# Linear attention followed by a squared-ReLU FFN on one core: first k by hardware queues, transposes in pieces, q by whole rows, squares on two engines

## The chip, the cores and the metric

The kernel runs on one core of a Trainium2 chip. TensorE (PE) multiplies matrices, VectorE (DVE) and ScalarE (ACT) do the work on elements, GpSimd (POOL) issues the loads that cast fp32 to bf16, SyncE (SP) issues stores and crossbar transposes. The metric is the device time of one execution in microseconds.

## What is computed

For each of 8 batches and 8 heads, 576 positions of 64 values are projected to 128 features, and exp of plus and minus the projection gives 256 features. The attention is linear: keys and values are summed once, queries read the sum. The result, 4608 tokens of 512, goes through an FFN of width 2048 whose activation is the square of a ReLU.

```python
def phi(x):
    proj = np.einsum('bhsd,df->bhsf', x, w_phi)
    proj = proj - np.max(np.abs(proj), axis=-1, keepdims=True)
    return np.concatenate([np.exp(proj), np.exp(-proj)], axis=-1)
q_p, k_p = phi(q), phi(k)
kv = np.einsum('bhsf,bhsd->bhfd', k_p, v)
z = np.sum(k_p, axis=2)
num = np.einsum('bhsf,bhfd->bhsd', q_p, kv)
den = np.einsum('bhsf,bhf->bhs', q_p, z)[..., None] + 1e-06
# x = num / den, heads side by side: (4608, 512)
h = np.maximum(x @ w_in, 0.0)
out = (h * h) @ w_out
```

Inputs and output are fp32.

## The kernel before

**Work of one batch.** `attention(b)` works on one batch at a time. q, k and v come to SBUF as bf16 tiles `xq`, `xk`, `xv` (two buffers each) of 128 partitions; the first 512 positions of a head lie four to a partition, and the last 64 positions of all heads form a small extra part, "s". A tile holds 18 blocks of 128 columns. They are transposed into `kT` and `qT`: for batches 0 and 1 on TensorE (`pe_transposes`, L616, with a copy out of PSUM by VectorE or ScalarE, L439 or L441), for later batches by one crossbar DMA for a whole tile on SyncE's queue (`transposed`, L626).

k is projected in five groups (L642, in batch 0 L670, matmuls on 64 rows of the array in pairs), VectorE takes the largest magnitude (L722, L677) and ScalarE the two exponentials `kp` and `kn` (L728, L705). `em_ops` and `v_ops` put the factor of the maximum on v (L740, L747, L762, L766), and `kv_ops` sums keys times values on TensorE (L783, L788) and copies the sum to `kv`. For q, `qmax_ops` finds the maxima (L642 or L816, then L823), `q_ops` makes the features (L858, exponentials L873) in five chunks `c`, and `out_ops` multiplies by the sums (L888), scales (L900), divides (L908, L912) and transposes the result into `xT`, on TensorE in batch 0 (L928, L937) and by crossbar DMAs of four blocks later (L950).

**FFN.** Tokens go in nine chunks of 512: eight are the main parts of the batches, the ninth holds all the small parts (`xS`). `ffn_in` (first chunk: `ffn_in_small`, L1049) multiplies by w_in (L1038); `relu_sq` takes the ReLU out of PSUM on ScalarE (L1015) or VectorE (L1017) into one of four buffers `hr` and squares it on VectorE (L1024) into `h2`. `ffn_out` multiplies by w_out (L1103), a copy brings the result to one of three `ot` buffers, and SyncE stores it (L1121).

**What sets the order.** Nothing is scheduled on the chip. `Plan` collects all operations with what they read and write; `Machine.run` plays them through with a cost for each and a due time from the list `KEYS`, and the program then issues each engine's instructions in the order that came out. `pin` holds that order. Each engine executes its list strictly in order, SyncE and GpSimd too, so that an instruction that waits holds all behind it. `STATES` says for each operation that two engines can do which one does it (`plan.either`). `RELEASES` hold loads back until a ScalarE instruction has ended. `SLACK` is what the planner adds to the expected landing of a DMA. In the first 45 us, where the planner finds TensorE idle and a PSUM bank is free, matmuls on a zero tile `warm` fill the time (L1195); how many is fixed when the program is built.

**Loads.** All loads but w_phi are issued by GpSimd, which casts in the DMA: `load` (L512 main part, L520 small part), `load_q` (L532), the FFN weights L581 and L587. `load_q` reads each q row of 256 fp32 values in two halves of 128, for both pairs of positions `jj`, so that the blocks of one `jj` lie together:

```python
out=x[:, jj * 1024 + a * 256 : jj * 1024 + z * 256].rearrange("p (h x) -> p h x", x=128),
in_=q[b][2 * a : 2 * z, 0:512, :].rearrange("h (p j) d -> p h (j d)", j=4)[:, :, jj * 128 : jj * 128 + 128]))
```

In batch 0, a chunk of q then needs one half of the columns for all eight heads. Only w_phi comes by hardware queues, one half issued on SyncE and the other on ScalarE (L476).

## Time and profile before

| what | value |
|---|---|
| time, three runs | 361.73, 362.86, 364.84 us; median 362.86 |
| profiled execution | 362.49 us, its span 360.4 us |
| mean granted TensorE clock | 0.986 |
| busy: PE, DVE, ACT, POOL | 346.7, 292.5, 231.9, 112.5 us |
| DMA packets under 512 bytes | 77249 of 102632 |
| SyncE's instructions: whole transposes of q and k, 4-block ones of xT, small ones of xS | 12, 28, 7 |

The span runs from the first to the last instruction of the profiled execution. "Busy" counts the time in which at least one instruction of the engine was in progress; matmuls are pipelined and overlap, so a busy TensorE isn't one that does as much as it could. The groups give the sum of busy time of like instructions, the mean of one, and the engine's idle time just before them with what ended it. The granted clock is the share of TensorE's full clock that it was given.

### The profile page before, as it was taken

Reading aid. Unit: us, or ns where it says so; the run is one execution under the profiler, and the core shown is the slowest. Engines: PE = TensorE matmul, PEld = TensorE weight load, DVE = VectorE, ACT = ScalarE, POOL = GpSimd, SP = SyncE. Lnnn points to the kernel's source line nnn. Section 1 sums busy time; section 2 is a strip of 40 time slices with the busy share of each in tenths; the row PEclk is TensorE's granted clock in tenths of the full one; section 3 lists DMA queues with packets and bytes.
Section 4 is the critical chain, followed back from the end, with each engine's and each line's share of the span. In section 5 each row is a group of like instructions: output and inputs, shape, how many; then the busy total and the mean of one; then the engine's idle time right before and its main releaser. Section 6 shows DMA issues by size and latency. Waiting matters only on the chain.

```text
span 360.4 us, 8594 instructions
## 1 busy us (share of the span) xinstructions
PE 346.7 (96%) x3442; PEld 198.0 (55%) x3442; DVE 292.5 (81%) x503; ACT 231.9 (64%) x434; POOL 112.5 (31%) x167
## 2 busy tenths in 40 slices
PE   8579999999999999999999999999999999999995
PEld 8368886554554555446544555565455554444444
DVE  4998999899999977899789888999788965686131
ACT  2986899598888783959677847957785340310310
POOL 8626727366636951363415212010000000000000
PEclk9959999999999999999999999999999999999999
DMA  8999999998999999898847774447230031100213
GB/s 96 194 201 136 188 182 117 169 150 107 164 154 126 153 129 188 167 139 121 98 102 96 128 98 104 93 69 122 81 96 2 17 95 45 36 0 2 112 33 89
DMA packets 102632, 39.62 MB, mean 110 GB/s; under 512 B 77249, under 2 KB 98113, under 8 KB 102593
## 3 DMA queue, kind: packets, MB, share of 16 engines
q0 software_dynamic: 51744, 18.36, 47.3%
q1 hardware_dynamic: 50608, 20.55, 25.4%
q8 instruction: 27, 0.44, 0.5%
q10 hardware_dynamic: 240, 0.16, 0.2%
q14 instruction: 13, 0.10, 0.1%
HBM read 36.77 MB, written 9.44 MB: 128 GB/s over the span
## 4 chain that ended last, share of the span: by engine, by line
PE 75%; DVE 11%; ACT 9%; issue 2%; DMA 1%; POOL 0%; DVEq 0%; POOLq 0%; ACTq 0%
PE psum L1103 29%; PE psum L1038 24%; PE psum L888 5%; PE psum L783 4%; DVE mq L823 4%; PE psum L642 3%; PE psum L858 3%; PE psum L1049 2%; ACT kp L728 2%; DVE mk L722 2%; DVE va L766 2%; ACT kn L728 2%; DMA xq<-in_q_dram 1%; DVE h L1024 1%; PE psum L1067 1%
## 5 line engine op out<-in xcount | busy, mean ns | idle before, releaser
L1103 PE MATMUL psum<-wout,h 128*128 128x512 bf16 x560 | 131.5, 379 | 0.0
L1038 PE MATMUL psum<-xT,win 128*128 128x512 bf16 x448 | 105.0, 379 | 0.6 <-ACT hr L1015 0.4
L1015 ACT ACTIVATE hr<-psum 128x512 bf16<-128x512 f32 x91 | 53.6, 598 | 49.7 <-PE psum L1038 26.1
L1103 PEld LDWEIGHTS <-h 128*128 128x128 bf16 x560 | 50.7, 98 | 56.9 <-issue 2.7
L1038 PEld LDWEIGHTS <-win 128*128 128x128 bf16 x512 | 47.5, 98 | 53.6 <-issue 1.6
L1024 DVE TENSOR_TENSOR h<-hr 128x512 bf16<-128x512 bf16 x144 | 56.9, 416 | 16.2 <-ACT hr L1015 15.3
L873 ACT ACTIVATE qp<-psum 128x1024 bf16<-128x1024 f32 (+1 forms) x40 | 37.3, 938 | 20.0 <-PE psum L858 17.4
L532 POOL DMA_DIRECT2D xq<-in_q_dram x52 | 37.6, 726 | 39.1 <-ACT hr L1015 10.3
L823 DVE TENSOR_REDUCE mq<-psum 128x8 f32<-128x1024 f32 (+1 forms) x40 | 43.7, 1110 | 4.6 <-PE psum L642 3.7
L1017 DVE TENSOR_SCALAR hr<-psum 128x512 bf16<-128x512 f32 x53 | 36.1, 683 | 9.8 <-PE psum L1038 8.3
L722 DVE TENSOR_REDUCE mk<-psum 128x8 f32<-128x1024 f32 (+1 forms) x35 | 38.1, 1108 | 2.4 <-PE psum L642 1.7
L728 ACT ACTIVATE kp<-psum 128x1024 bf16<-128x1024 f32 (+1 forms) x35 | 32.8, 937 | 10.2 <-DVE mk L722 10.2
L766 DVE TENSOR_TENSOR va<-xv,va 128x1024 bf16<-128x1024 bf16 (+1 forms) x36 | 38.6, 1101 | 0.6 <-ACT va L747 0.4
L873 ACT ACTIVATE qn<-psum 128x1024 bf16<-128x1024 f32 (+1 forms) x40 | 37.4, 940 | 2.0 <-PE psum L888 2.0
L900 DVE TENSOR_TENSOR psum<-psum,en 128x520 f32<-128x520 f32 (+1 forms) x40 | 27.9, 700 | 7.4 <-PE psum L888 6.4
L728 ACT ACTIVATE kn<-psum 128x1024 bf16<-128x1024 f32 (+1 forms) x35 | 32.9, 948 | 0.1
L912 DVE TENSOR_TENSOR xo<-psum,rden 128x512 bf16<-128x512 f32 (+1 forms) x40 | 27.3, 687 | 0.9
L512 POOL DMA_DIRECT2D xv<-in_v_dram x26 | 18.9, 727 | 28.9 <-ACT qp L873 10.5
L512 POOL DMA_DIRECT2D xk<-in_k_dram x28 | 20.2, 721 | 21.9 <-ACT va L747 7.4
L783 PE MATMUL psum<-va,kp 128*128 128x65 bf16 x256 | 21.1, 199 | 0.1
L783 PE MATMUL psum<-va,kn 128*128 128x65 bf16 x256 | 20.9, 198 | 0.1
L441 ACT ACTIVATE ot<-psum 128x512 f32<-128x512 f32 x24 | 14.4, 603 | 10.0 <-PE psum L1103 6.8
(68 smaller groups left out, 407.4 us busy)
## 6 DMA issues: line engine op xcount, KB each, us to landing
out_dram<-ot SPq DMA_DIRECT2D x32, 256.0 KB, 2.6
xk<-in_k_dram POOLq DMA_DIRECT2D x26, 128.0 KB, 4.4
xv<-in_v_dram POOLq DMA_DIRECT2D x24, 128.0 KB, 4.4
xq<-in_q_dram POOLq DMA_DIRECT2D x48, 64.0 KB, 3.4
win<-in_moe_w_in_dram POOLq DMA_DIRECT2D x4, 512.0 KB, 11.0
wout<-in_moe_w_out_dram POOLq DMA_DIRECT2D x4, 512.0 KB, 7.7
xq<-in_q_dram POOLq DMA_DIRECT2D x4, 256.0 KB, 7.5
xv<-in_v_dram POOLq DMA_DIRECT2D x2, 512.0 KB, 8.5
```

Source lines behind the costliest of these rows:

```text
L512: pin(nc.gpsimd.dma_start(out=x[:, a * 512 : z * 512].rearrange("p (h x) -> p h x", x=4 * D), in_=src[b][2 * a : 2 * z, 0:512, :].rearrang ...
L532: pin(nc.gpsimd.dma_start(out=x[:, jj * 1024 + a * 256 : jj * 1024 + z * 256].rearrange("p (h x) -> p h x", x=128), in_=q[b][2 * a : 2 * z ...
L722: pin(nc.vector.tensor_reduce(out=mk_view(g), in_=ps2(pj)[:, :, : n * Fd].rearrange("p e (i f) -> p e i f", f=Fd), axis=AX.X, op=ALU.max, ...
L728: pin(nc.scalar.activation(out=dst[slot][:, :, :n, :].rearrange("p e i f -> p e (i f)"), in_=ps2(pj)[:, :, : n * Fd], func=ACT.Exp, scale= ...
L766: pin(nc.vector.tensor_tensor(out=o[:, :, :D], in0=xv[s2][:, 512 * g0 : 512 * g1].rearrange("p (m d) -> p m d", d=D), in1=o[:, :, D].to_br ...
L783: pin(nc.tensor.matmul(out=o[:, sg, hi, :], lhsT=(kp, kn)[sg][kgroup[pr]][:, j % 2, 2 * hi + j // 2, :], rhs=va[s2][sg_of(sg, pr)][:, 8 * ...
L823: pin(nc.vector.tensor_reduce(out=mqb[:, c, :, :n], in_=ps2(pj)[:, :, : n * Fd].rearrange("p e (i f) -> p e i f", f=Fd), axis=AX.X, op=ALU ...
L873: pin(nc.scalar.activation(out=o, in_=i_, func=ACT.Exp, scale=sgn))
L1015: pin(nc.scalar.activation(out=hr[sl], in_=ps1(g), func=ACT.Relu))
L1024: pin(nc.vector.tensor_tensor(out=dst, in0=i_, in1=i_, op=ALU.mult))
L1038: pin(nc.tensor.matmul(out=o, lhsT=win[mc // 4][:, kc, mc % 4 * P : (mc % 4 + 1) * P], rhs=x, start=(kc == 0), stop=(kc == KC - 1)))
L1103: pin(nc.tensor.matmul(out=ps1(g), lhsT=h2[c % 2][mc // 4][:, mc % 4, tt * P : (tt + 1) * P], rhs=wout[mc // 4][:, mc % 4, :], start=(mc = ...
```

## The change

**First k.** Batch 0's k groups 0 and 1 and its small part are copied as fp32 by hardware queues into the three `ot` buffers, which are not in use yet; three copies on VectorE or ScalarE cast them into `xk`. SyncE issues group 0, one half of w_phi and the small part, ScalarE group 1 and the other half of w_phi. GpSimd loads only groups 2 and 3 of that k.

**q by whole rows.** `load_q` is gone; q is loaded by `load` as k is, in rows of 256 values, so block `2 * h + jj` belongs to head `h`. `q_ts` and the views of `qT` step by two blocks. A chunk of q in batch 0 now needs both halves of the q load, in which the halves are heads 0 to 3 and 4 to 7.

**Transposes in pieces.** `transposed` issues five crossbar DMAs for a tile, four of four blocks and one of two, each waiting for its own part of the load. Batch 1's q goes this way too, and is no longer transposed on TensorE (`PE_Q`).

**Squares.** The square in `relu_sq` may be done by ScalarE.

**Planner.** PSUM bank 7 is kept free until 27 us of the planner's time, so fill matmuls can stand wherever TensorE is idle there. `SLACK` is smaller, limits and patience are others, and `KEYS`, `STATES` and `RELEASES` are new lists. By the built programs, 69 of the 144 squares are on ScalarE; VectorE has 8 more copies of key-value sums, 5 more of `ot` and 5 more ReLUs; the fill matmuls are 210 instead of 118; GpSimd issues 24 main loads of q in place of 48 for batches 2 to 7; SyncE's transposes of q and k are 65 instead of 12.

```diff
-SLACK = {"first": 1.2, "v0": 2.5, "ld": 0.8, "x": 1.2, "kq": 1.0}
+SLACK = {"first": 0.6, "v0": 1.0, "ld": 0.6, "x": 0.8, "kq": 1.0}
...
-        self.free_at = [0.0] * self.BANKS
+        self.free_at = [0.0] * (self.BANKS - 1) + [RESERVED]
...
+            if name == "PE" and t < RESERVED:
+                spare = self.BANKS - 1
...
+    kf = {0: ot[0], 1: ot[1], "s": ot[2]}
...
+    def first_k(g, name, e, lat):
+        def fn():
+            pin(e.dma_start(
+                out=kf[g].rearrange("p (h x) -> p h x", x=4 * D),
+                in_=k[0][2 * g : 2 * g + 2, 0:512, :].rearrange("h (p j) d -> p h (j d)", j=4)))
+        first_ops.append(add(name, (0.6, lat), -10, fn, w=[("ot", g)], what="xk"))
...
+    first_k(0, "SP", nc.sync, 2.9)
+    first_w(1, "ACT", nc.scalar)
+    first_w(0, "SP", nc.sync)
+    for hi in range(2):
+        first_s(hi, "SP", nc.sync, 3.0)
+    first_k(1, "ACT", nc.scalar, 3.6)
+
+    for n, g in enumerate((0, 1, "s")):
+        def fn(g=g):
+            if g == "s":
+                copy(xk[0][:, 2048:2304], kf[g][:, :256])
+            else:
+                copy(xk[0][:, g * 512 : g * 512 + 512], kf[g])
+        x = 256 if g == "s" else 512
+        o = add("DVE", dve_cost(x), -9 + n * 0.1, fn, r=[("ot", n)],
+                w=[("xk", 0, "s", hi) for hi in range(2)] if g == "s" else [("xk", 0, g)], what="kc")
+        plan.either((o, "ACT", act_cost(x)))
...
-            def fn():
-                pin(nc.sync.dma_start_transpose(out=xt, in_=x))
-            add("SP", (2.8 if tag == "xk" else 3.4, 0), key, fn, r=of(tag, b, (0, 1, "s") if tag == "xq" else (0, 1, 2, 3, "s")),
-                w=[(ttag, s2, t) for t in range(18)], dma=(3.6, HW_IN, "x", "kq"), what="X" + tag)
+            def piece(a, n, srcs):
+                def fn():
+                    pin(nc.sync.dma_start_transpose(out=xt[:, a : a + n, :], in_=x[:, a * P : (a + n) * P]))
+                add("SP", (1.23, 0), key + a * 0.1, fn, r=of(tag, b, [u for u in srcs if u == "s"]) + [t for t in srcs if t != "s"],
+                    w=[(ttag, s2, t) for t in range(a, a + n)], dma=(0.2 * n, HW_IN, "x", "x"), what="X" + tag)
+            for g in range(4):
+                piece(4 * g, 4, [(tag, s2, g)])
+            piece(16, 2, ["s"])
...
-            return [8 * (c // 2) + h for h in range(8)] if first else [8 * (c // 2) + 4 * (c % 2) + i for i in range(4)]
+            return [2 * h + c // 2 for h in (range(8) if first else range(c % 2 * 4, c % 2 * 4 + 4))]
...
-            pin(nc.vector.tensor_tensor(out=dst, in0=i_, in1=i_, op=ALU.mult))
-        add("DVE", dve_cost(256), key, fn, r=[("hr", sl)], w=toks, what="sq")
+            if now[0].eng == "ACT":
+                pin(nc.scalar.activation(out=dst, in_=i_, func=ACT.Square))
+            else:
+                pin(nc.vector.tensor_tensor(out=dst, in0=i_, in1=i_, op=ALU.mult))
+        o = add("DVE", dve_cost(256), key, fn, r=[("hr", sl)], w=toks, what="sq")
+        plan.either((o, "ACT", act_cost(512)))
...
-    load(k, xk, 0, -9, "xk", prs=((0, 1),))
...
-    load(k, xk, 0, -8, "xk", prs=((1, 2), (2, 4)), single=False)
-    load_q(0, -7.5, jjs=(0,), single=False)
+    load(k, xk, 0, -8, "xk", prs=((2, 4),), single=False)
+    load(q, xq, 0, -7.5, "xq", prs=((0, 2), (2, 4)))
     load_v0(-7)
-    load_q(0, -6, jjs=(1,))
...
-    load_q(1, -3.9)
+    load(q, xq, 1, -3.9, "xq", prs=((0, 2), (2, 4)) if 1 not in K["PE_Q"] else ((0, 4),))
...
-                load_q(b, r, release=max(r, 1.0), prs=PIECES)
+                load(q, xq, b, r, "xq", prs=PIECES, release=max(r, 1.0))
...
+    'PE_Q': [0],
...
-    'LIM': {'b0': 7, 'att': 3, 'kv': 7, 'op': 6},
-    'AHEAD': 356.131,
-    'PATIENCE': 60.701,
+    'LIM': {'tp': 6, 'att': 6, 'kv': 6, 'op': 4},
+    'AHEAD': 168.898,
+    'PATIENCE': 15.023,
```

## The prediction

> **What bounds the kernel now.** I read the busy shares first, then the stretches of ten microseconds, then the timeline of the start, and only then the groups.
>
> ```profile
> PE 346.7 (96%) x3442; PEld 198.0 (55%) x3442; DVE 292.5 (81%) x503; ACT 231.9 (64%) x434; POOL 112.5 (31%) x167
> ...
> PE   8579999999999999999999999999999999999995
> ...
> PEclk9959999999999999999999999999999999999999
> ```
>
> TensorE is busy almost everywhere, except in the first tenth. But pipelined matmuls overlap in this view, so I counted its work by start-to-start distances in dense stretches of the trace: 0.216 us for 512 columns, 0.056 for 128, 0.0295 for 65, 0.057 for 130, 0.109 for 256; matmuls on 64 rows run in pairs at half of that. 1072 of 512 columns in the two FFN layers are 231.6 us, the 256 small ones of the first chunk 14.3, the last 32 3.5; the attention's 512 and 64 of its key-value sums 18.7, its 640 output matmuls 18.9, projections and features 25, transposes 5. A change between 64-row and full matmuls costs 0.095 more (89 of them, from 60 us on: 0.092 to 0.096), and the order has 112: 10.6. The sum is 327.5 us. The last matmul ends at 356.4, so **28.9 us are TensorE's idle time**, and only that and the 4 us behind it can change much.
>
> ```profile
> 0.00:10.00 10.00, 8.79 (x104) 8.07 (x105) 5.01 (x12) 3.35 (x5) 8.92 (x17) 1.00 0.95 105
> 10.00:20.00 10.00, 5.19 (x75) 3.66 (x72) 9.50 (x17) 9.96 (x25) 6.03 (x9) 0.81 1.44 197
> 20.00:30.00 10.00, 8.43 (x138) 7.55 (x138) 8.83 (x15) 7.93 (x21) 3.14 (x5) 0.67 1.32 175
> 30.00:40.00 10.00, 10.00 (x199) 9.30 (x197) 9.64 (x25) 7.23 (x13) 7.71 (x11) 1.00 1.24 159
> ```
>
> The columns are PE, PEld, DVE, ACT, POOL, granted clock, DMA. Most of the 8.79 in the first row is fill work. From 10 to 20 ScalarE has no free moment and VectorE hardly any; from 20 to 30 the clock is at 0.67. By single microseconds it is 0.50 from about 16.4 to 26.7, after four (13 to 17) with TensorE busy 0.90, 0.00, 0.40 and 0.26.
>
> ```profile
> 2.70 5.38 DMA xq<-in_q_dram
> ...
> 7.70 0.60 ACT L705 ACTIVATE kp<-psum 128x512 bf16<-128x512 f32 x1 [5.07 <-PE psum L670]
> ...
> 27.51 0.39 ACT L441 ACTIVATE kv<-psum 128x260 bf16<-128x260 f32 x1
> ...
> 33.20 0.61 PE L1049 MATMUL psum<-xT,win 128*128 128x128 bf16 x8
> ```
>
> These four rows, one from the chain of waits and three from the timeline, are the start: ScalarE's first exponential at 7.70, the last key-value copy at 27.51 (done 27.9), the first FFN matmul at 33.20. TensorE's work ahead of that matmul adds up to about 12.3 us, so **21 us of the 28.9 lie ahead of it, 8 behind**. From there TensorE is dense.
>
> **The change part by part.** Work: batch 1's q is no longer transposed on TensorE, 18 x 0.056 = 1.0 us less. The changed program's order has 122 changes of mode instead of 112: 10 x 0.095 = 1.0 more. The two cancel. Ahead of the first FFN matmul the new order has 12.6 us of real work instead of 12.3, no difference worth a term. So all turns on idle time.
>
> *First k by hardware queues.* Before, k's first 128 KB piece was issued on GpSimd at 2.00 and used at 6.25. Now 256 KB of fp32 start on SyncE and on ScalarE's queue at 0.74. Nearest rows: hardware copies of 256 KB land 2.6 us after issue, w_phi's 32 KB in 2.1 to 2.5; a software load of 256 KB takes 5.8 and is the other end. I take 2.9: 3.6 us. w_phi is now second on both queues (0.58 each), so its cast (0.39, done about 4.2) stands ahead of the k casts in VectorE's order. An fp32 cast of 512 columns is not in the trace; bounds are a quarter-size cast at 0.39 and a 512-column fp32 copy at 0.69; I take 0.6, behind idle VectorE (3.67 to 6.73 before), except for the first, which is on the path: 4.8. Four cold transposes (0.107 each) and latency: ScalarE starts the kT copies at about 5.4 (4.8 to 7.7 by the ends).
>
> *ScalarE's list up to the last key-value copy* in the new order: 16 exponentials of 512 at 0.475 start to start, 7 of 1024 at 0.90, 4 of 256 at 0.27, 7 copies at 0.49, 12 small ones at 0.155, 3 key-value copies at 0.28, 3 of 8 columns at 0.16: 21.6 us. 5.4 + 21.6 = 27.0. The second half of k and the q halves still come by GpSimd; among its loads they stand third, fifth and sixth, and I add 0.5 for one of them being late: 27.5, against 27.9. The gain is small since before, a part of the list came later.
>
> *From there to the first FFN matmul* it took 5.3 us. VectorE's order there held a qT copy, a maximum and a kT copy (0.2 + 0.6 + 0.33) between the scalings and the xT copies; the new order has none of them: 4.2, so 31.7. **Ramp: 33.2 - 31.7 - 0.3 (more work done) = 1.2, and 0.6 for the half clock**: the 64 key-value matmuls took 2 us more than at full clock (1.05 per pair for 0.55), partly on the path; now 210 fill matmuls instead of 118, 89 of them in the two stretches where TensorE stood idle, should hold the clock. If it falls all the same, these 89 take 0.107 instead of 0.056 each, 4.5 us on the path. Ends: no gain if k lands like a software load; 3.7 if nothing is late and ScalarE starts at 4.8.
>
> *Squares on ScalarE.* 69 of 144 move; 51 stand ahead of the last batch's exponentials.
>
> ```profile
> L1024 DVE TENSOR_TENSOR h<-hr 128x512 bf16<-128x512 bf16 x144 | 56.9, 416 | 16.2 <-ACT hr L1015 15.3
> L1015 ACT ACTIVATE hr<-psum 128x512 bf16<-128x512 f32 x91 | 53.6, 598 | 49.7 <-PE psum L1038 26.1
> ```
>
> A square costs 0.416 on VectorE; on ScalarE the nearest row is the relu of that size, 0.598. VectorE loses 69 x 0.416 = 28.7 and gains about 11 (8 key-value copies, 5 ot copies and 5 relus more, fewer transposes' copies): 292 to 275. ScalarE goes from 232 to about 262. Between 40 and 110 us VectorE is busy 78 to 100% and TensorE idles 3.4 by the count above; with both engines near 80%, I take 2.5 of the 8 us back, with ends of 6 gained and 3 lost (a square that waits behind exponentials of 1.03). By these rows a square is 1.4 times dearer on ScalarE, which had 128 us free. The Trainium skill, page "ScalarE: Activation LUTs", "Rules for kernel authors", speaks against this part: multiplications belong on VectorE, up to about three times faster in bf16; by that ratio the 69 squares would cost 57 us more engine time than they do now. One table load stands in the built program before and after, so Square costs no reload.
>
> *Whole q rows.* In the trace's DMA records a 256-byte packet takes 41 ns, a 512-byte one 60: the q data of one batch saves 27% of its DMA time. It is hidden after 46 us, and helps the loads of the start (DMA at 1.2 to 1.4 there). I cost it at nothing.
>
> *Crossbar pieces.* A whole q or k transpose holds SyncE 3.1 us and lands after 5.2 to 6.5; one of four blocks, as xT has it, 1.2 and 2.6. A tensor goes from 3.1 to 4 x 1.20 + 1.17 = 6.0 us of SyncE, 13 tensors instead of 12: 78 instead of 37, with 42 for xT and xS. SyncE has the room. The same skill's "DMA: Bandwidth & Descriptors", "Bandwidth", warns that small transfers are descriptor-dominated; it measured loads, no row here shows that for transposes. Every piece waits in SyncE's order for its part of a load, and stores and xT transposes stand behind it. Before, such a wait reached 3.6 us (at 58.5) with TensorE covered by FFN work.
>
> **Sum.** Ramp -1.8, steady idle -2.5, work 0: 360.4 - 4.3 = 356.1 of span. Around it lie 2.1 us (362.49 - 360.4): **358.2 us**. The profiled run stands 0.4 below the median, 362.86.
>
> **Rivals.** *The start gives more* (0.17): ScalarE starts at 4.8, no load is late (3.7), and balanced engines leave TensorE 2 of its 8 us: 362.5 - 3.7 - 6 = 353. For it: VectorE 81%, ScalarE 64%. Against it: TensorE already dense behind 33 us.
> *It moves and nothing comes of it* (0.28): k early, but the q halves and k's second half, still on GpSimd behind 512 KB of v, hold ScalarE as long; the steady gain is 1: 361.5. For it: 5.38 us for q in the chain; DMA at 1.4.
> *SyncE's queue becomes the bound* (0.14, slower): 65 pieces wait in order; where a load is over some 4 us late, the xT transposes behind it start the next chunk late, and TensorE's FFN backlog runs out. At 2 us in each of five batches, 10 us: 358.2 + 10 = 368. Against it: no TensorE wait on a DMA after 20 us in the list of waits.
> *The forecast* has 0.41, from 355 to 360.5.
>
> The measurement tells about 1% (3.6 us) from no change. Faster by more than that is all of the first rival and most of the forecast: 0.54; within: 0.32; slower: 0.14. The range leaves out the best end and most of the slow rival: 353 to 366.
>
> **What would show it.** Right: first exponential at about 6, clock 1.0 from 16 to 27, first FFN matmul at 31 to 32, VectorE near 275 and ScalarE near 262 us, no TensorE wait on xT. Wrong: loads of q or k in the chain beyond 10 us, a half clock with the longer fill, an idle stretch of TensorE between 60 and 290 that xT ends, or ScalarE as the releaser of most waits.

## The result and the profile after

The changed kernel takes 375.03 us, the median of four runs (372.89 to 377.88), against 362.86 before: a ratio of 1.0334, 95% interval 1.0251 to 1.0418. I had forecast 358.2. The profiled execution took 374.58 us with a span of 372.8. Times here are medians of all executions of a kernel, while the ratios leave out single executions that ran in a slower state.

The first lines are of the profile page of the changed kernel: busy times, then TensorE and its clock in 40 slices.

```profile
PE 354.8 (95%) x3516; PEld 201.7 (54%) x3516; DVE 277.6 (74%) x448; ACT 261.8 (70%) x487; POOL 92.7 (25%) x139
...
PE   4699899999999999989999999999999999999995
...
PEclk9599999999999999999999999999999999999999
```

VectorE and ScalarE came out as forecast (277.6 and 261.8 us; 275 and 262), and TensorE's work hardly changed. What changed is its idle time. Counted by start-to-start distances in both traces, with 0.11 us for a change between 64-row and full matmuls, it is 28.0 us before and 40.6 after (the prediction summed the work with 0.095 and had 28.9 before), and these 12.6 us are the whole difference. By stretch: up to 40 us it idles 29.4 us instead of 21.8, from there to the end 11.2 instead of 6.2. The stretches of ten microseconds (PE, PEld, DVE, ACT, POOL, granted clock, DMA, GB/s):

```profile
0.00:10.00 10.00, 4.53 (x43) 4.10 (x43) 3.29 (x9) 0.00 (x0) 6.53 (x13) 0.91 0.86 141
10.00:20.00 10.00, 7.62 (x93) 7.23 (x93) 2.86 (x7) 7.42 (x15) 4.87 (x7) 0.57 1.37 200
20.00:30.00 10.00, 9.71 (x159) 7.99 (x157) 9.78 (x17) 9.74 (x27) 2.71 (x4) 1.00 1.20 162
30.00:40.00 10.00, 9.02 (x160) 6.73 (x157) 9.00 (x13) 9.95 (x18) 6.56 (x10) 1.00 1.27 161
```

In the first ten microseconds ScalarE does nothing at all, although the DMA moves more than before (141 GB/s, 105 before). The half clock, forecast to go, only moved: 0.57 from 10 to 20 and 1.00 from 20 to 30, where it was 0.81 and 0.67. The reason is in the timeline of the start:

```profile
5.20 0.28 DVE L517 CAST wphi<-wphi_f 128x128 bf16<-128x128 f32 x1 [2.00 <-DMA wphi_f<-in_w_phi_dram]
5.41 0.94 DVE L441 CAST xk<-ot 128x512 bf16<-128x512 f32 x2
...
10.62 1.28 ACT L443 ACT_TABLE_LOAD   x1 [10.62 <-DMA ot<-in_k_dram]
11.91 0.42 ACT L443 ACTIVATE xk<-ot 128x256 bf16<-128x256 f32 x1
12.23 1.06 ACT L443 ACTIVATE kT<-psum 128x512 bf16<-128x512 bf16 x2
13.92 0.60 ACT L734 ACTIVATE kp<-psum 128x512 bf16<-128x512 f32 x1 [0.62 <-PE psum L699]
...
36.09 0.47 ACT L443 ACTIVATE kv<-psum 128x260 bf16<-128x260 f32 x1
...
41.92 1.95 PE L1082 MATMUL psum<-xT,win 128*128 128x128 bf16 x32
```

and in the list of DMA issues (how many, KB each, us from issue to landing):

```profile
ot<-in_k_dram SPq DMA_DIRECT2D x1, 256.0 KB, 3.3
ot<-in_k_dram ACTq DMA_DIRECT2D x1, 256.0 KB, 3.8
ot<-in_k_dram SPq DMA_DIRECT2D x2, 64.0 KB, 8.0
```

The two large pieces of k were in at 4.1 and 4.5 us, for 3.6 forecast. w_phi, second on both queues, was in at 5.0 and 5.2, and its cast, which stands ahead of theirs in VectorE's order, ended at 5.48 instead of 4.2; so k was cast by 6.4. Worse, the two copies of the small part, 64 KB each in rows of 256 bytes, took 8.0 us, longer than four times as much data in rows of 1024 bytes. ScalarE's first instruction in the new order is the cast of that part; it waited until 10.62, the table load of 1.28 us stood behind the same wait (before, it ran at 1.35, hidden), and so did the kT copies of the large pieces, whose transposes on TensorE had begun at 6.4. Before, the first exponential came at 7.70, now at 13.92; the first FFN matmul at 33.20, now at 41.92. Of the 12.4 us by which the span grew, 8.7 lie ahead of that matmul and 3.7 behind it.

### The profile page after: what moved, and what is told of

The parts are those of the page before. It is cut to its first block, busy times and chain, and to the rows that moved or that the text cites. A ratio compares the mean times of both kernels' runs of the same rounds, so it can differ in the third digit from the quotient of the medians.

```text
span 372.8 us, 8807 instructions
## 1 busy us (share of the span) xinstructions
PE 354.8 (95%) x3516; PEld 201.7 (54%) x3516; DVE 277.6 (74%) x448; ACT 261.8 (70%) x487; POOL 92.7 (25%) x139
## 4 chain that ended last, share of the span: by engine, by line
PE 64%; DMA 11%; ACT 10%; DVE 6%; issue 4%; POOL 2%; SPq 1%; POOLq 0%; ACTq 0%; DVEq 0%
PE psum L1136 25%; PE psum L1071 24%; PE psum L917 4%; DMA xq<-in_q_dram 3%; PE psum L671 3%; DMA ot<-in_k_dram 2%; PE psum L812 2%; DVE va L795 2%; ACT qp L902 2%; PE psum L887 2%; DMA xk<-in_k_dram 2%; DMA out_dram<-ot 2%; ACT hr L1044 2%; ACT qn L902 1%; DVE mq L852 1%
## 5 line engine op out<-in xcount | busy, mean ns | idle before, releaser
L1044 ACT ACTIVATE hr<-psum 128x512 bf16<-128x512 f32 x86 | 50.0, 596 | 26.2 <-PE psum L1071 18.1
L1046 DVE TENSOR_SCALAR hr<-psum 128x512 bf16<-128x512 f32 x58 | 39.4, 684 | 25.8 <-PE psum L1071 12.8
L1054 ACT ACTIVATE h<-hr 128x512 bf16<-128x512 bf16 x69 | 43.1, 633 | 9.6 <-DVE hr L1046 8.7
L902 ACT ACTIVATE qp<-psum 128x1024 bf16<-128x1024 f32 (+1 forms) x40 | 37.3, 936 | 14.2 <-PE psum L887 13.3
L1056 DVE TENSOR_TENSOR h<-hr 128x512 bf16<-128x512 bf16 x75 | 30.5, 416 | 9.6 <-ACT hr L1044 9.0
L549 POOL DMA_DIRECT2D xq<-in_q_dram x28 | 20.2, 722 | 42.5 <-ACT qp L902 21.5
L549 POOL DMA_DIRECT2D xk<-in_k_dram x26 | 18.8, 724 | 36.3 <-ACT qp L902 7.5
L557 POOL DMA_DIRECT2D xq<-in_q_dram x16 | 10.2, 636 | 50.1 <-ACT hr L1044 22.3
L443 ACT ACTIVATE ot<-psum 128x512 f32<-128x512 f32 x19 | 11.2, 595 | 15.9 <-PE psum L1136 15.9
## 6 DMA issues: line engine op xcount, KB each, us to landing
win<-in_moe_w_in_dram POOLq DMA_DIRECT2D x4, 512.0 KB, 11.3
```

Source lines behind the costliest of these rows:

```text
L549: pin(nc.gpsimd.dma_start(out=x[:, a * 512 : z * 512].rearrange("p (h x) -> p h x", x=4 * D), in_=src[b][2 * a : 2 * z, 0:512, :].rearrang ...
L902: pin(nc.scalar.activation(out=o, in_=i_, func=ACT.Exp, scale=sgn))
L1044: pin(nc.scalar.activation(out=hr[sl], in_=ps1(g), func=ACT.Relu))
L1046: pin(nc.vector.tensor_scalar(out=hr[sl], in0=ps1(g), scalar1=0.0, scalar2=None, op0=ALU.max))
L1054: pin(nc.scalar.activation(out=dst, in_=i_, func=ACT.Square))
L1056: pin(nc.vector.tensor_tensor(out=dst, in0=i_, in1=i_, op=ALU.mult))
```

## The experiments

Each run changes the program after the planner has set its order, so that everything not named keeps its place. All are compared with runs of the kernel before on the same chip. My theory after seeing the result was that the start is the loss, because the small part comes late beside other transfers (A); its rivals were that its 512 short packets are slow by themselves (B), and that the loss lies in the order or in other parts of the change (named where they are tested).

### The small part and the table load

`e1_small_first` puts the small part's copies first, one on each hardware queue; `e2_table_early` runs an exponential of 8 columns ahead of ScalarE's first wait; `e3_both` does both; `e4_both_squares_dve` also gives all squares back to VectorE.

```diff
 # e1
-first_s(hi, "SP", nc.sync, 3.0)
+first_s(hi, "SP", (nc.sync, nc.scalar)[hi], 3.0)
+order = small + [op for op in order if op not in small]
 # e2, behind ScalarE's DMA issues
+pin(nc.scalar.activation(out=tl, in_=warm[:, :8], func=ACT.Exp))
 # e4
+for op in order:
+    if op.what == "sq":
+        op.eng = "DVE"
```

> The changed kernel, with the two copies of the first k's small part issued first, one on SyncE and one on ScalarE, ahead of the large k copies; every other instruction stays in its place. In the changed kernel they were issued at 1.9 and 2.6 us and landed 8.0 us later, and ScalarE's first instruction, the cast of this part, waited until 10.6. Theory A (they lost the DMA engines to GpSimd's 512 KB load of v, which began at 3.9): ahead of that load they land by about 4, ScalarE's cast starts at about 5.5 and the first exponential at about 8 instead of 13.9; the time falls by 5 to 7 us, to about 368. Theory B (copies in 256-byte packets are slow by themselves, whatever runs beside them): they still land after 7, the large k copies behind them come later too, and the time stays at 375 or grows.

> The changed kernel, with one more instruction on ScalarE: an exponential of 8 zeros right after its two DMA issues, ahead of the cast that waits. It draws the table load (1.28 us, at 10.6 in the changed kernel, behind the wait) to the start. If ScalarE's list is what sets the time of the start, the first exponential comes at 12.6 instead of 13.9 and the time falls by 1.3 us, to about 373.7. If something else is as late (q or the other half of k), nothing is gained: 375.

> Both edits: the small part first, and the table load early. Theory A: first exponential at about 6.5, the time falls by 7 to 9 us, to 366 to 368; the 4 us that are left over the kernel before are then those of the later stretches (50 to 180 us), where TensorE idled about 4.6 us more than before. Rival C (the start matters little, since TensorE has idle time to give before its FFN work; the loss is made by SyncE's 65 pieces and the late loads of the second batch): less than 3 us gained, 372 or more.

> As e3, and all 144 squares on VectorE again, each at its place in the order. If the split of the squares helps as forecast, this is 2 to 6 us slower than e3: 28.7 us go back to VectorE, which is then at 305 us or more. If squares in ScalarE's order hold exponentials back more than they help, it is faster than e3.

Measured: 373.46 us (1.0273, 1.0221 to 1.0325), 373.18 (1.0259, 1.0209 to 1.0308), 372.28 (1.0229, 1.0206 to 1.0252) and 381.51 (1.0504, 1.0475 to 1.0533). The small part is early when it stands first, but then others are late. The DMA issues of `e1_small_first`, then its timeline:

```profile
ot<-in_k_dram ACTq DMA_DIRECT2D x1, 256.0 KB, 5.5
ot<-in_k_dram SPq DMA_DIRECT2D x1, 64.0 KB, 2.6
wphi_f<-in_w_phi_dram SPq DMA_DIRECT2D x1, 32.0 KB, 6.6
```

```profile
4.68 0.42 ACT L443 ACTIVATE xk<-ot 128x256 bf16<-128x256 f32 x1
...
9.07 0.23 DVE L517 CAST wphi<-wphi_f 128x128 bf16<-128x128 f32 x1 [5.86 <-DMA wphi_f<-in_w_phi_dram]
10.66 1.09 ACT L443 ACTIVATE kT<-psum 128x512 bf16<-128x512 bf16 x2 [5.57 <-PE psum L639]
```

64 KB land 2.6 us after issue here, with 18 ns a packet in the DMA records, instead of 8.0 with 31 ns. So the slow landing is no property of the copy: it is its place, behind other copies and beside GpSimd's software loads, whose first large packets start at about 4 us. Which of the two weighs more, this run doesn't tell. Now w_phi, 32 KB, needs 6.6 us and holds VectorE's list, where the casts of k stand behind it, and the first exponential comes at 12.41. In the changed kernel and these runs, what stands last on these queues is in at 9 to 10.7 us. The changed order needs all of it, 704 KB of fp32, ahead of its first exponential; the order before needed one piece of k, 256 KB of fp32, and w_phi. The early table load by itself brings the first exponential forward by 1.1 us; beside the small part first it brings nothing (13.02 in `e3_both`, 12.41 in `e1_small_first`), since w_phi is later still. Both mends together gain 2.8 of the 12 us.

### Who else uses the DMA engines

`e5_soft_later` is `e3_both` with GpSimd's list reordered: the mask and small loads first, v's 512 KB last.

```diff
-# GpSimd: v, v small, q, v small, k's rest, mask, q
+# GpSimd: mask, v small, v small, q, k's rest, q, v
```

> The kernel with the small part first and the table loaded early, and GpSimd's list changed at its head: the mask, the two small loads of v, then half of q, k's rest, the other half of q, and the 512 KB of v only then (it was first). Theory C (the hardware copies of k and w_phi are slow because GpSimd's loads take the DMA engines beside them): the first large software packets start at about 5 to 6 us instead of 3.9, so k, the small part and w_phi are all in by 5.5 us (512 KB took 2.2 us where nothing ran beside), the first exponential starts at 7 to 8 instead of 13.0, the first FFN matmul at 34 to 36 instead of 39.6, and the time falls from 372.3 to 366 to 369. Rival D (the hardware queues are slow by themselves when 704 KB stand on them): w_phi still lands at 8 to 9, the first exponential stays at 12 to 13, 371 to 374. A third case: the start is early, but v, now last, is late for the key-value sums, and the gain at the exponentials is gone at the first FFN matmul: 371 to 373 with a first exponential before 8.

Measured: 371.34 us (1.0214, 1.0194 to 1.0235), first exponential at 11.59. The casts of k:

```profile
7.84 0.47 DVE L518 CAST wphi<-wphi_f 128x128 bf16<-128x128 f32 x1 [4.63 <-DMA wphi_f<-in_w_phi_dram]
7.98 1.16 DVE L442 CAST xk<-ot 128x512 bf16<-128x512 f32 x2
```

w_phi's cast comes 1.8 us earlier than in `e3_both` (9.68), not 4, and the first exponential is nearer to D's forecast than to C's. So GpSimd's large loads are a part of the delay. What makes the rest isn't shown: 640 KB stand ahead of w_phi on its queues, but v's small loads (512 packets of 128 bytes) also run beside it.

From there on ScalarE waits for no load in this run. Its first kT copy, its last copy of key-value sums and the first FFN matmul:

```profile
9.84 1.09 ACT L444 ACTIVATE kT<-psum 128x512 bf16<-128x512 bf16 x2 [5.33 <-PE psum L640]
...
31.98 0.47 ACT L444 ACTIVATE kv<-psum 128x260 bf16<-128x260 f32 x1
...
37.82 1.39 PE L1083 MATMUL psum<-xT,win 128*128 128x128 bf16 x22
```

The list takes 22.6 us, against 24.3 in the changed kernel.

### First k by GpSimd again, and the order of its loads

`e6_k_gpsimd` takes part one of the change out of the changed order: casting loads on GpSimd at the head of its list, no fp32 copies, no casts; it keeps the early table load. `e9_q_before_v` and `e16_v_middle` move v's 512 KB behind q, and between q's halves.

```diff
+order = [op for op in order if op not in hw and op.what != "kc"]     # without hardware copies and casts
+order = [cast_load(0), cast_load(1), cast_small(0), cast_small(1)] + [op for op in order if op is not mask]
 # the mask then behind "ident0", the early table load as in e2
 # e9: GpSimd then issues q, k's rest, q, v, v small, v small
 # e16: GpSimd then issues q, v small, v small, v, k's rest, q
```

> Part one of the change undone within the changed order: all of k's first pieces come by GpSimd's casting loads again, at the head of its list (two of 256 KB, two small), with the mask behind them; the casts on VectorE and ScalarE are gone; w_phi is alone on the hardware queues; the table is loaded early. If loading by the hardware queues is the loss (theory A/C), k lands at about 7.5 to 8.5, the first exponential at 9 to 10 (13.9 in the changed kernel, 7.7 before), and the time is 368 to 371 against 375 of the changed kernel. If the loss lies elsewhere in the new order (rival E: the order, whose plan has other landing times, or the pieces), the start is earlier but the time stays at 372 to 375. GpSimd's other loads are issued 2.9 us later here, which may cost up to that where q or v is late.

> The run with k by GpSimd in the changed order (370.0), with one edit: behind the mask GpSimd issues half of q, k's rest and the other half of q, and only then v's 512 KB and its two small parts (v stood first). There ScalarE's first exponential came at 7.4 but it then stood 3.3 us for q and k's rest, and the first FFN matmul came at 37.2. If the start is the loss (theory A), those waits go, the first FFN matmul comes at 33.5 to 35 and the time is 366 to 368. What stays above the 362.6 of the kernel before is then the later part of the order (its pieces of crossbar transposes and its loads), 3 to 5 us. If v, issued 3 us later, is late for VectorE's scalings, the first FFN matmul stays at 36 to 37 and the time at 369 to 371.

> The changed order with k by GpSimd, and the rest of its loads in the order half of q, the two small parts of v, v's 512 KB, k's rest, the other half of q. With v first VectorE had v in time but ScalarE stood 3.3 us for q and k's rest (370.0; first FFN matmul at 37.2); with v last VectorE stood 2.9 us for v (371.7; 36.9). If what the changed order needs is simply all of k, q and v by some 12 us, which no order of GpSimd's list can give, the first FFN matmul stays at 36 to 38 and the time at 368 to 372. If it was only the order of the loads, 34 to 35 and 366 to 368.

Measured: 370.02 us (1.0209, 1.0189 to 1.0229), 371.73 (1.0198, 1.0134 to 1.0262) and 371.33 (1.0241, 1.0204 to 1.0278). With k by GpSimd the first exponential is at 7.41, earlier than before the change, and 4.7 us of the 12.2 are gone (370.02 is 7.5 above the kernel before in the same comparison). But the first FFN matmul still comes at 37.23 instead of 33.20. And `e5_soft_later`, with k still by hardware queues and its first exponential 4.2 us later (11.59), has its first FFN matmul at 37.82 and a ratio that can't be told from this one (1.0214 and 1.0209, on the same chip). So it isn't the hardware route as such that costs the 4.7 us: it is that route in the sequence of loads that the change gave it. Nor does an early first exponential alone bring the FFN forward. ScalarE's timeline in `e6_k_gpsimd`:

```profile
7.41 1.36 ACT L735 ACTIVATE kp<-psum 128x512 bf16<-128x512 f32 x3 [0.54 <-PE psum L700]
...
12.84 0.60 ACT L444 ACTIVATE qT<-psum 128x512 bf16<-128x512 bf16 x1 [1.28 <-PE psum L640]
15.45 0.60 ACT L444 ACTIVATE kT<-psum 128x512 bf16<-128x512 bf16 x1 [2.02 <-PE psum L640]
...
26.00 0.39 ACT L444 ACTIVATE kv<-psum 128x260 bf16<-128x260 f32 x1
...
30.30 1.10 ACT L758 ACTIVATE kp<-psum 128x1024 bf16<-128x1024 f32 x1
31.40 0.47 ACT L444 ACTIVATE kv<-psum 128x260 bf16<-128x260 f32 x1
```

It stands 3.3 us for q and k's rest, which now come later. Moving v back does not mend it: then VectorE stands 2.9 us for v (`e9_q_before_v`; first FFN matmul at 36.9), and with v in the middle ScalarE stands 5.1 us for k's rest (`e16_v_middle`; 40.1). None of the three orders of GpSimd's list that were tried brings all of k, q and v by the time at which this order uses them. Also, between ScalarE's first and last copy of key-value sums 5.4 us pass here (26.00 to 31.40), with an exponential of batch 1 among them; before, 1.5 (25.98 to 27.51).

### Each part alone, in the order of before

`e12_before_hw_k` puts k on the hardware queues in the kernel before (k first, w_phi second, the small part last, since that order needs it last); `e15_before_wphi_first` has w_phi first. `e7_before_pieces` issues each whole crossbar transpose as five pieces, `e14_before_halves` as two; unlike in the change, all pieces of a tensor stand together, behind its whole load. `e8_before_squares` gives every second square to ScalarE. `e18_before_both` is `e15` with halves.

```diff
 # e12: SyncE k0, w_phi, small; ScalarE k1, w_phi, small; three casts on VectorE
+order = [op for op in order if op not in pieces]      # GpSimd's loads of these parts
+head = [op_of("SP", "hk", hw_k(0, nc.sync)), op_of("ACT", "hk", hw_k(1, nc.scalar)), wp["SP"], wp["ACT"],
+        op_of("SP", "hs", hw_s(0, nc.sync)), op_of("ACT", "hs", hw_s(1, nc.scalar))]
 # e7, e14
-pin(nc.sync.dma_start_transpose(out=xt, in_=x))
+for a, n in ((0, 4), (4, 4), (8, 4), (12, 4), (16, 2)):      # e14: ((0, 9), (9, 9))
+    pin(nc.sync.dma_start_transpose(out=xt[:, a : a + n, :], in_=x[:, a * P : (a + n) * P]))
 # e8
+for op in [op for op in order if op.what == "sq"][::2]:
+    op.eng = "ACT"
```

> The kernel before, with part one of the change alone: k's first two pieces come by the hardware queues in fp32, first on SyncE's and ScalarE's queues, w_phi second, the small part last, cast on VectorE; GpSimd's list loses these four loads, so q and v are issued 2.9 us earlier. The order of the engines is that of before, in which the first exponential needs only the first piece and w_phi, and the small part is needed last. My prediction's step about this part: cast done at 4.8, first exponential at about 6 (7.7 before), 1 to 4 us gained: 359 to 362. Rival: with GpSimd's loads issued earlier beside them, w_phi and k are late as in the changed kernel (w_phi landing at 8 to 9), the first exponential comes at 9 to 11 and the time is 364 to 368.

> As the run of before with k by the hardware queues (362.7, no difference; there w_phi stood behind k's 256 KB on both queues, was in at 5.3 instead of 3.1, and the first exponential came at 7.96), but with w_phi first on both queues and k second. If w_phi behind k was what ate the gain of part one, the casts end at about 5.0, the first exponential comes at 6.3 to 7.2 instead of 7.7, and the time is 361 to 362.3. If an earlier first exponential is worth nothing in this order (ScalarE and VectorE then wait for q, which GpSimd brings), 362.5 to 363.3 with a first exponential before 7.3. If k second is as late: first exponential at 7.7 to 8.5 and no difference.

> The kernel before, with one edit: each whole crossbar transpose of a q or a k is issued as four of four blocks and one of two, in the same place of SyncE's order. My prediction's step (SyncE has the room, nothing waits): 362 to 364, no difference. Rival (the pieces hold SyncE for 6.0 us instead of 3.1 and the stores and xT transposes behind them are late, or 65 pieces cost DMA time): 366 to 372, with xT as the releaser of idle time on TensorE.

> The kernel before, each whole crossbar transpose issued as two of nine blocks instead of four of four and one of two. If the loss of the run with five pieces (13.0 us) comes from the time that SyncE is held (about 3.0 us for the whole, 6.5 for five pieces), then the two halves, some 3.6 to 4 us by these rows, cost a small part of it: 363 to 366. If it comes from a piece landing later than a whole, or from any change of this order, the loss is nearly as large with two: 368 to 375.

> The kernel before, with one edit: every second square (72 of 144) is done by ScalarE, in its place in the order by time. My prediction's step: 2.5 us gained, 359 to 362, VectorE near 263 us busy, ScalarE near 276. Rival F (in an order made for squares on VectorE, a square on ScalarE stands behind exponentials and comes late for the second layer): 364 to 372. Beside the run that put the squares of the changed order back (9.2 us lost) this tells whether the split is worth something by itself or only in an order made for it.

> The kernel before with w_phi first and k second on the hardware queues, and with each whole crossbar transpose in two halves (0.9984 by itself): the version that the runs so far point to. 361 to 362.5 if both small gains add, 362.5 to 363.2 if they were nothing.

| run | us | ratio, 95% interval |
|---|---|---|
| `e12_before_hw_k` | 362.72 | 0.9999 (0.9983 to 1.0015) |
| `e15_before_wphi_first` | 363.06 | 1.0002 (0.9985 to 1.0018) |
| `e7_before_pieces` | 375.59 | 1.0383 (1.0319 to 1.0446) |
| `e14_before_halves` | 362.53 | 0.9984 (0.9966 to 1.0003) |
| `e8_before_squares` | 370.92 | 1.0221 (1.0193 to 1.0250) |
| `e18_before_both` | 363.23 | 1.0006 (0.9989 to 1.0024) |

**First k** is worth nothing by itself, with w_phi first or second. The timeline of `e12_before_hw_k`:

```profile
5.38 0.23 DVE L480 CAST wphi<-wphi_f 128x128 bf16<-128x128 f32 x1 [2.18 <-DMA wphi_f<-in_w_phi_dram]
5.53 0.97 DVE L1211 CAST xk<-ot 128x512 bf16<-128x512 f32 x2
7.96 0.60 ACT L705 ACTIVATE kp<-psum 128x512 bf16<-128x512 f32 x1 [4.14 <-PE psum L670]
```

k is there, but w_phi, which it has overtaken, is cast at 5.38 instead of 3.28; with w_phi first, k's first cast runs from 4.79 to 5.22 and the first exponential is at 7.59. Either way it is about the 7.70 of before. By the trace TensorE began the first piece's transposes only at 6.18 (6.55 in `e12_before_hw_k`), right behind the second cast, although they read only the first; so these two runs show that the route as built gains nothing, and not what an earlier exponential would be worth. With halves as well (`e18_before_both`) nothing is gained either.

**Pieces** cost 13 us by themselves. SyncE's timeline, first before, then with five pieces, then with two:

```profile
136.99 3.29 SPq L626 DMA_TRANSPOSE qT<-xq  x1
...
141.82 2.99 SPq L626 DMA_TRANSPOSE qT<-xq  x1
```

```profile
143.89 6.49 SPq L627 DMA_TRANSPOSE qT<-xq  x5
150.47 1.22 SPq L951 DMA_TRANSPOSE xT<-xo  x1
151.79 6.49 SPq L627 DMA_TRANSPOSE qT<-xq  x5
```

```profile
136.57 3.52 SPq L627 DMA_TRANSPOSE qT<-xq  x2
141.67 2.84 SPq L627 DMA_TRANSPOSE qT<-xq  x2
```

The chain of waits of `e7_before_pieces` at the same place:

```profile
153.10 3.63 DMA qT<-xq
...
156.77 0.42 PE psum L643 x8
157.19 1.09 SPq L627
...
158.99 1.23 SPq L951
...
160.90 5.54 DMA xT<-xo
```

and two lines of TensorE's list of waits there (us in total, times, longest), which had no wait on a transpose before:

```profile
PE psum L643 <- DMA qT<-xq: 4.9, 2, 2.9
PE psum L1039 <- DMA xT<-xo: 2.6, 4, 1.0
```

Over the whole run transposes of q and k hold SyncE 37.3 us before, 36.0 with halves and 76.9 with five pieces. One of nine blocks holds it 1.34 us at the median, one of four 1.21, one of two (`e17_after_twos`, below) 1.20: from nine blocks down the time hardly falls with the size. Two halves are free; five pieces hold it twice as long, and the store and the xT transposes behind them are late, so that TensorE waits for qT, then for xT. A single xT transpose lands no later with five pieces (3.1 us from issue at the median) than with two (3.2). The two waits make 7.5 of the 13 us; the rest isn't put down to a cause.

**Squares** cost 8.4 us by themselves, although VectorE was 81% busy and ScalarE 64%. The groups of ReLUs on VectorE (busy, mean ns, then idle before and what ended it), before and in `e8_before_squares`:

```profile
L1017 DVE TENSOR_SCALAR hr<-psum 128x512 bf16<-128x512 f32 x53 | 36.1, 683 | 9.8 <-PE psum L1038 8.3 <-ACT hr L1015 0.9
```

```profile
L1025 ACT ACTIVATE h<-hr 128x512 bf16<-128x512 bf16 x72 | 45.5, 633 | 20.6 <-DVE hr L1017 19.6
L1017 DVE TENSOR_SCALAR hr<-psum 128x512 bf16<-128x512 f32 x53 | 36.2, 686 | 27.0 <-PE psum L1041 13.8 <-ACT h L1025 11.3 <-ACT hr L1015 1.0
```

There are four `hr` buffers. A square that waits its turn on ScalarE keeps its buffer, and VectorE's next ReLU waits for it: 11.3 us that were not there before. That this wait makes the 8.4 us fits these lines, but no run separates it from squares that come late for the second layer. In the changed order the same wait is 12.2 us (of 25.8 idle at L1046), and yet taking the split away there costs 9.2 us (`e4_both_squares_dve` against `e3_both`). So these runs give the split no price of its own: in either order it costs 8 to 9 us to leave the assignment that the order was made for.

### Pieces within the changed order

`e17_after_twos` issues each piece of four as two of two in the changed kernel. `e13_merged` (on `e9_q_before_v`) joins pieces that follow one another in SyncE's order; `e19_pairs_k_gpsimd` (on `e6_k_gpsimd`) and `e20_after_pairs` (on the changed kernel) join 18 pairs of four blocks into one of eight from batch 2 on.

```diff
 # e17
-pin(nc.sync.dma_start_transpose(out=xt[:, a : a + n, :], in_=x[:, a * P : (a + n) * P]))
+for i in range(a, a + n, 2):
+    pin(nc.sync.dma_start_transpose(out=xt[:, i : i + 2, :], in_=x[:, i * P : (i + 2) * P]))
 # e19, e20: the earlier or the later of the two places, as readers and loads allow
+keep.fn = merged(p0, a0, 8)
+order.remove(gone)
```

> The changed kernel with each piece of four blocks issued as two of two blocks: 9 transposes of a q or k instead of 5, so that what pieces cost in this order is nearly doubled. If pieces are hidden in the order made for them (my prediction's step, SyncE has the room), 375 to 376. If SyncE's time ends the work here as it does in the order of before (13 us for going from 1 to 5, nothing for going from 1 to 2), each tensor holds SyncE for some 10.6 us instead of 6: 380 to 395.

> The kernel with k by GpSimd and q ahead of v, with one edit more: where pieces of the same q or k follow one another in SyncE's order and hold neighbouring blocks, they are issued as one transpose (seven merged pieces in place of nineteen). If the time that pieces hold SyncE is part of the loss (what the run of before with pieces, 13 us slower, suggests), 1 to 3 us are gained against the run without it. If in this order the pieces were hidden, as I predicted, no difference within 1 us; if the merged ones wait for their last block's load and hold up those behind, slower.

> The run with k by GpSimd in the changed order (370.0), and from batch 2 on two neighbouring pieces of four blocks (0 and 4, 8 and 12) are issued as one of eight, wherever no reader or load stands between them: 18 of 24 pairs, 47 transposes instead of 65. A piece of nine blocks held SyncE 1.34 us and one of four 1.2, so SyncE is held some 19 us less. If the pieces' hold is part of what the changed order loses, 2 to 5 us are gained: 365 to 368. If it is not (only the start and the order of work), 369.5 to 371. If the pairs, which wait for the later of two loads, hold up what stands behind, slower: 371 to 375 (as with the merged pieces of the first batches, 4 us slower).

> The changed kernel itself (375.0) with the same 18 pairs as its only edit. Same theories: 370 to 373 if the pieces' hold on SyncE is a part of the 12 us, 374.5 to 376 if not, more if the pairs wait for their later load.

Measured: 403.6 us (1.1125, 1.1083 to 1.1166), 376.11 (1.0350, 1.0325 to 1.0375), 374.84 (1.0331, 1.0273 to 1.0389) and 378.31 (1.0419, 1.0383 to 1.0455). More pieces cost 28.6 us: 117 transposes hold SyncE 151.8 us instead of 85.1. The longest lines on transposes in TensorE's list of waits, in the changed kernel, in `e17_after_twos` and in `e20_after_pairs`:

```profile
PE psum L1071 <- DMA xT<-xo: 1.1, 1, 1.1
```

```profile
PE psum L1072 <- DMA xT<-xo: 10.2, 5, 4.0
PE psum L672 <- DMA qT<-xq: 6.4, 3, 4.3
```

```profile
PE psum L673 <- DMA kT<-xk: 5.6, 2, 4.3
```

But fewer pieces, joined in this order, gain nothing: `e13_merged` and `e19_pairs_k_gpsimd` are 4.4 and 4.8 us slower than the runs that they build on, `e20_after_pairs` 3.3 slower than the changed kernel with intervals that overlap. A pair waits for the later of two loads, and in `e20_after_pairs` TensorE, whose order expects the first part early, stands for kT. So SyncE has no room for more transposes in the changed order, while it is not shown that its five pieces are a part of the 12 us.

## Why the prediction was wrong, point by point

**What bounds the kernel: right.** TensorE's idle time is the account in which the change shows, 12.6 us more of it for 12.2 us more time.

**First k by hardware queues: the step that failed.** I took 2.9 us for the 256 KB copies (3.3 and 3.8 measured) and 0.6 for a cast (0.41 to 0.60), both near. I said that w_phi and the casts set ScalarE's start, 5.4, and counted the small part nowhere: neither its landing of 8.0 us nor that ScalarE's first instruction, and with it the table load, waits for it. The start was 12.23, 6.8 us late. Some 1.4 of these come from w_phi, whose cast ended at 5.48 instead of 4.2, and the casts behind it (estimate: transposes at 6.40, and 0.43 to the first copy, as in `e6_k_gpsimd`); the other 5.4 are the small part and the table load. My bounds of 4.8 and 7.7 bounded only the large copies. What comes last on a queue beside other loads is not bounded by a row of a copy that ran alone.

The rest of that sum: ScalarE's list up to the last key-value copy took 24.3 us (12.23 to 36.56) for 21.6 and 0.5 forecast; from there to the first FFN matmul 5.4 us passed, for 4.2. With the 6.8 that is 10.2 us later than the 31.7 forecast: 41.9, as measured.

**The mended start is no gain either.** In `e6_k_gpsimd` ScalarE's kT copies start at 5.78, as good as the 5.4 forecast, and the first FFN matmul still comes 5.5 us after the 31.7. Two more terms of the sum were too small: the list took 26.1 us for 22.1, 3.3 of them waits for loads for which I had 0.5, and the stretch behind it 5.4 for 4.2, as in `e5_soft_later` and no shorter than the 5.3 before. The list itself was sized well: 22.6 us in `e5_soft_later`, where no load is late. With the best of each, 5.4 + 22.6 + 5.4 = 33.4 (an estimate from these rows), the first FFN matmul would come no earlier than the 33.20 of before. And k by hardware queues in the order of before is worth 0.0 us. So none of the runs shows the gain of 1.2 us for the ramp.

**Half clock: half right.** With the longer fill the clock is 1.00 from 20 to 30, but TensorE stood for the small part from 7.0 to 12.4 and the clock was 0.57 from 10 to 20.

**Squares: sizes right, sign not what was claimed.** VectorE and ScalarE came out within 3 us; a square on ScalarE took 0.633 us for 0.598. I gave -2.5 for the balance of busy times. In the order of before the split costs 8.4, in the changed one its removal costs 9.2; behind 40 us TensorE idles 5.0 us more with all parts together, not 2.5 less. My lower case, a square that is late on ScalarE, fits the groups, through the four buffers; I had put its price at 3.

**Crossbar pieces at nothing: wrong as a step.** I had the right hold (78 us forecast, 85.1 measured) and the wrong reading, "SyncE has the room": the sum of the holds says nothing of three tensors close together with xT transposes between and behind them (6.96, 6.49 and 6.49 us of holds between 136.8 and 158.3 us in `e7_before_pieces`). In the order of before that costs 13.0 us; whether it is a part of the changed kernel's loss stays open. The Trainium skill, "DMA: Bandwidth & Descriptors", "Bandwidth", calls transfers under 64 KB descriptor-dominated. A piece of four blocks is 128 KB, and what the runs show is another cost: some 1.2 us of the issuing queue for each transpose of up to four blocks.

**Rivals.** The slower one (368, SyncE's queue) has its mechanism shown in two runs, `e7_before_pieces` and `e17_after_twos`, which have more transposes than their orders were made for. But of the 12.4 us more of span, 8.7 are there at the first FFN matmul, and the start I had only with gains. "Nothing comes of it" named GpSimd's loads as what holds ScalarE; it was a hardware copy, and only with that mended were it GpSimd's loads (3.3 us in `e6_k_gpsimd`).

**The account of the 12.2 us.** In the forecast's own terms the span of 356.1 is missed by 16.7 us: 10.2 up to the first FFN matmul, 6.5 behind it (330.9 us for 324.4; before, 327.2). 4.7 us of the loss go with k's way by the hardware queues as the change orders it (`e6_k_gpsimd`, which also has the early table load). Of the 7.5 left, 4.0 are there at the first FFN matmul: by the traces that order uses k, q and v earlier than any list of loads tried delivers them. The other 3.5 lie behind, in many small waits; no run shows one cause. It stays open what whole q rows alone would do, since the layout reaches through all batches. No version here beats the kernel before: the best are equal to it.

## What to carry to other kernels

When a load changes its queue, list everything that its first consumers wait for, down to the smallest piece, and what stands behind that wait in the consumer's order; price the last of them, not the first; and when that wait is mended, look for the one that was hidden behind it. An engine that only issues is not free because its sum is small: look at the longest run of holds ahead of something urgent, and split a transfer only down to where the hold stops falling. A part that moves work between two engines has no price outside the order it was planned in, so measure it in both.

## What was not expected of the hardware

- A hardware copy of 64 KB in rows of 256 bytes: 2.6 us from issue to landing when first (18 ns a packet), 8.0 when behind 288 KB on its queue and beside a software load (31 ns); the two conditions were not separated. The Trainium skill, "DMA: Bandwidth & Descriptors", "Queues, rings and completion order", says that each DMA engine takes turns between the queues it has work for, a packet at a time. The records agree as far as they go: between 5.1 and 10.1 us the 512 packets of the small part start among 1199 of 512 bytes of the software loads; which engine took which isn't recorded.
- The activation table load is placed ahead of ScalarE's first activation. In the changed kernel that activation waits for two copies; in the trace one of the two waits is an instruction of its own ahead of the table load (it ends at 10.58), so the load ran at 10.62 instead of 1.35. In the kernel before, the first activation has a single wait, its own, until 7.70, and the load ran ahead of it; with an activation of a single short wait put first it ran at 1.87. The skill's "ScalarE: Activation LUTs", "Step-by-step: what each stage is for", states the place; that a wait can stand ahead of it, only these runs show.
- A crossbar transpose holds SyncE 1.2 us for two or four blocks, 1.34 for nine, 3.1 for eighteen. Seven of four or two blocks in a row beside other loads (from 33.3 us in the changed kernel, 13.4 us in all) follow one another every 1.9.
